# First four heads: operands that stay on their partitions are written by ScalarE instead of copied by DMA

## The chip, the cores and the metric

The kernel runs on one core of a Trainium2 chip. The metric is the time of one execution in microseconds of device time; a kernel's time is the median of several executions. In one core the engines run side by side, each in the order of its own instructions: TensorE (PE, its weight loads shown as PEld), VectorE (DVE), ScalarE (ACT), GpSimd (POOL) and SyncE (SP), which here mainly issues DMA transfers. They wait for one another by semaphores. SBUF, the working memory, and PSUM, into which TensorE writes, have 128 partitions.

## The reference

Three stages follow one another. The change lies in the first, a bucketed attention over 2 batches x 8 heads, 768 positions, head dimension 64:

```python
def _attn_ref(q, k, v, proj):
    q_bits = (einsum('bhsd,dk->bhsk', q, proj) > 0)     # 6 bits
    k_bits = (einsum('bhsd,dk->bhsk', k, proj) > 0)
    mask = q_bucket[:, :, :, None] == k_bucket[:, :, None, :]
    scores = scale * matmul(q, k.transpose(0, 1, 3, 2))
    scores = where(mask, scores, -1e9); scores -= max(scores)
    attn = exp(scores); attn /= attn.sum(-1) + 1e-9
    return matmul(attn, v)
...
def reference(...):
    x = _attn_ref(...)       # 1536 x 512 after the heads are put side by side
    x = _moe_ref(x, ...)     # 8 experts, top 1, 512 -> 1024 -> 512
    return _moe2_ref(x, ...) # 512 -> 2048 -> 512 with a leaky relu
```

## The kernel before

The order of every engine is the order in which the program is written; nothing reorders it. A prologue brings up heads 0, 1 and 2, then a loop of 102 steps runs attention, with the work of later heads spread over its steps by the tables in PLAN (a step runs scores and sums, and at its end the pieces that the tables put there). Then come the experts and the last stage.

Each head has an operand tile OP[h%NP] of 128 partitions x 4 planes x 768 columns; NP is 5, so heads 0 to 3 have a tile that no earlier head used. The scores and the masks come out of it by matmuls over its partitions:

- `load(h)` (L621) brings k and q of a head side by side into `raw[h]`, by two transfers.
- `T(h, half)` (L721) transposes three blocks of 128 positions on TensorE into a PSUM tile `misc` of 128 x 384 (k on partitions 0 to 63, q on 64 to 127). ScalarE writes it, scaled and rounded, to `A[h]` (L728). `T2` (L730) follows at once: VectorE writes the rest, the tile less A, to `B[h]` (L732). There are two `misc` buffers in all, for T, Z, POSTb and a few others.
- `OD(h, n0, n1)` (L738) copies A and B into the operand tile by DMAs that SyncE issues (L617): k's A into planes 0 and 1 of partitions 0 to 63 in one transfer, q's A into plane 2 of partitions 0 to 63 and plane 3 of partitions 64 to 127, k's B into plane 0 of partitions 64 to 127, q's B into plane 3 of partitions 0 to 63. Two of these five, the first and the third, leave the data on the partitions it has; the others move it between the halves.
- `Z` (L742) and, for head 0 alone, `Z0` (L761) compute the bits by three matmuls for each half; VectorE turns them into signs (L755, L769). For Z they go into the operand tile by DMA, for Z0 VectorE writes them there.
- `MAX(u, a)` (L771) is a matmul from planes 2 and 1 and a VectorE reduction (L776) of its row, two for each of the six blocks of a head. `POSTa` and `POSTb` turn the maxima into a row that ScalarE's own DMA queue puts into plane 2 (`op<-mr`, L789).
- `ST(s, a)` (L796) computes the scores by two matmuls (L803, L804), and ScalarE takes the exponential.

GpSimd clears partitions 64 to 127 of planes 1 and 2 of each operand tile ahead (L667, L668).

In the prologue the order is T(0), Z0, T(1), the remaining copies of head 0, MAX of head 0 with Z of head 1 between, POSTa and POSTb, the first ST, T(2), MAX of head 1; T(3) comes at loop step 2, together with Z of head 3 and T(4,0).

Of the kernel before, what the change touches and what calls it, by code (L numbers as in the profile page):

```python
# [13 lines left out]
AF = mybir.ActivationFunctionType  # L14
# [4 lines left out]
SC = 2.0 ** -15  # L19
EPS = 1e-9  # L20
G = 2
NP = 5
# [18 lines left out]
    98, 100, 101), vl=1, am0=(0, 0, 0, 1), Z2=(0, 1), first=(75, 79),  # L41
)
NPRE = 3
NT = 22
NBASE = 13
EH_DVE = ()
# [9 lines left out]
class Router:  # L56
# [5 lines left out]
    def constants(self, w_gate, mbias, mod):  # L62
# [74 lines left out]
        self.rm = P([128, 12], F32, "rm")  # L137
        self.ids = P([128, NT], I32, "ids")
        self.gc = P([128, NT], F32, "gc")
        self.idp = P([128, NPRE], I32, "idp")  # L140
        self.gp = P([128, NPRE], F32, "gp")
        self.did = P([128, 12], I32, "did")
# [153 lines left out]
    def star2(self):  # L296
# [9 lines left out]
        v.tensor_reduce(out=self.m0, in_=k, axis=AX.X, op=ALU.add)  # L306
        v.tensor_scalar(out=self.m0, in0=self.m0, scalar1=128.0 * NPRE, scalar2=None, op0=ALU.min)
        yield
# [15 lines left out]
    def adjust(self, b):  # L324
# [4 lines left out]
        if b == 0:  # L329
            pf = self.tmp([128, 6], F32, "pf")  # L330
            v.scalar_tensor_tensor(out=pf, in0=self.r[:, bs], scalar=128.0 * NPRE, in1=self.isS[:, bs], op0=ALU.is_lt, op1=ALU.mult)
            yield
# [9 lines left out]
    def pre(self, ps):  # L342
# [4 lines left out]
        v.scalar_tensor_tensor(out=q, in0=self.np_[:, 0:6], scalar=100.0, in1=self.rq[:, 0:6], op0=ALU.mult, op1=ALU.add)  # L347
        s = [128, 6, NPRE]
        rc = self.tmp(s, F16, "prc")
        v.tensor_tensor(out=rc, in0=self.iota[:, 0:NPRE].unsqueeze(1).to_broadcast(s), in1=q.unsqueeze(2).to_broadcast(s), op=ALU.is_equal)  # L350
        yield
# [29 lines left out]
    def experts(self):  # L381
# [4 lines left out]
        v.tensor_tensor(out=en, in0=sd[0:1, 0], in1=nt[0:1, 0], op=ALU.add)  # L386
        s = [1, NT, 8]
        it = self.iota[0:1, 0:NT]
        a = self.tmp(s, F32, "xa")
# [4 lines left out]
        v.tensor_tensor(out=a, in0=a, in1=self.iota[0:1, 0:8].unsqueeze(1).to_broadcast(s), op=ALU.mult)  # L394
        et = self.tmp([1, NT], F32, "et")
        v.tensor_reduce(out=et, in_=a, axis=AX.X, op=ALU.add)
        v.tensor_copy(et[:, 0:NPRE], self.es[0:1].to_broadcast([1, NPRE]))
        info = self.info = self.pp.tile([1, 2 * NT + 1], I32, tag="info", name="info")
        v.tensor_copy(info[:, 0:NT], et)
# [74 lines left out]
def _program(base, tc, nc, q, k, v, proj, mod, w_gate, mbias, w1, w2, win, wout, alpha, out):  # L474
# [141 lines left out]
    def f32(ap): return ap.bitcast(F32)  # L616
    def dma32(o,i): nc.sync.dma_start(out=f32(o),in_=f32(i))  # L617
    mm=nc.tensor.matmul
    def misc():
        return ps1.tile([128,512],F32,tag="misc",name="misc",bufs=PS[2])  # L620
    def load(h):  # L621
        b,hh=divmod(h,8)
        t=raw[h]=BIG[2][:,h%3*768:h%3*768+768].rearrange("p (c a d) -> p c a d",c=6,a=2)
        for cs in (slice(0,3),slice(3,6)) if h==0 else (slice(0,6),):
            nc.sync.dma_start(out=t[:,cs,0],in_=k[b,hh].rearrange("(p c) d -> p c d",p=128)[:,cs])
            nc.sync.dma_start(out=t[:,cs,1],in_=q[b,hh].rearrange("(p c) d -> p c d",p=128)[:,cs])
# [20 lines left out]
    for i in range(G):  # L647
        for s in range(2):
            ps=slice(64*s,64*s+64)
            o=pw[ps,i,24*i+12*s:24*i+12*s+12].rearrange("p (a b) -> p a b",a=2)  # L650
# [13 lines left out]
    OP=[]  # L664
    for i in range(NP):
        t=slot16(i)[:,0:3072].rearrange("p (a n) -> p a n",a=4); OP.append(t)
# [45 lines left out]
    def later(f,p):  # L712
        if now[0]: f()
        else: todo.append((p,f))
# [3 lines left out]
    def defer(f,k):  # L718
        if LAGS[k] and not now[0]: dq.append(f)
        else: f()  # L720
    def T(h,half):  # L721
        if half==0:
            A[h]=ep.tile([128,768],F32R,tag="A",name="A",bufs=2); B[h]=ep.tile([128,768],F32R,tag="B",name="B",bufs=2)
        p=misc()
        for c in range(3):
            nc.tensor.transpose(p[:,c*128:(c+1)*128],raw[h][:,half*3+c].rearrange("p a d -> p (a d)"),ident)
        sl=slice(half*384,half*384+384)
        nc.scalar.activation(A[h][:,sl],p[:,0:384],AF.Copy,scale=SC)  # L728
        defer(lambda:T2(h,half,p),0)
    def T2(h,half,p):  # L730
        sl=slice(half*384,half*384+384)
        nc.vector.scalar_tensor_tensor(out=B[h][:,sl],in0=p[:,0:384],scalar=SC,in1=f32(A[h][:,sl]),op0=ALU.mult,op1=ALU.subtract)  # L732
        if half==1:
            if h!=1: OD(h,0,2)
            if h>1:
                OD(h,2,5)
                if 4<h+3<NH: later(lambda:load(h+3),2)
    def OD(h,n0,n1):  # L738
        t=OP[h%NP]; lo,hi=slice(0,64),slice(64,128)
        k2=A[h][lo].unsqueeze(1).to_broadcast([64,2,768])  # L740
        for o,i in (((lo,slice(0,2)),k2),((lo,2),A[h][hi]),((hi,3),A[h][hi]),((hi,0),B[h][lo]),((lo,3),B[h][hi]))[n0:n1]: later(lambda o=o,i=i:dma32(t[o],i),1)
    def Z(hs,half):  # L742
        n=24*len(hs); g=hs[0]
        if half==0: zb[g]=BIG[2][0:24*G,2304:3072]
        p=misc()
        sl=slice(half*384,half*384+384)
        for i,h in enumerate(hs):
            mm(p[0:n,0:384],pwh[:,i,0:n],A[h][:,sl],start=(i==0),stop=False)
            mm(p[0:n,0:384],pwh[:,i,0:n],B[h][:,sl],start=False,stop=False)
            mm(p[0:n,0:384],pwl[:,i,0:n],A[h][:,sl],start=False,stop=(i==len(hs)-1))  # L750
        defer(lambda:Z2(hs,half,p),1)
# [83 lines left out]
    def at(s,f): other.setdefault(s,[]).append(f)  # L835
    def sl_at(s,f): slot.setdefault(s,[]).append(f)
    T(0,0);T(0,1);Z0(0);Z0(1)
    T(1,0);T(1,1)
    OD(0,2,5)
    OD(1,0,2)  # L840
    load(2)
# [10 lines left out]
    for s in ahead[2:]: ST(s,0)  # L852
    load(4)
    T(2,0);T(2,1)
    for u in range(6,NU):
        for a in range(2): MAX(u,a)
# [23 lines left out]
    for s in range(96+LAG+2):  # L880
        us=[u for u in range(nu,min(96,s+6+LA+1,nu+(PLAN["cap"][s] if s<len(PLAN["cap"]) else 2)))]; nu+=len(us)
        fs=dq[:]; dq.clear()
        for o in ORDER:
            t=s-1-LAG
# [13 lines left out]
            t=s-LAG  # L898
# [336 lines left out]
    with ExitStack() as m2:  # L1235
# [64 lines left out]
        for s in range(50):  # L1300
            b, c = divmod(s, 16)
            p = QS[s] if s < 13 else None
# [69 lines left out]
```

## Time and profile before

| | |
|---|---|
| median of 3 runs | 754.55 us (754.51 to 758.52) |
| the profiled execution, its own time | 752.42 us |
| its span, first to last instruction | 750.6 us |
| TensorE busy | 697.3 us, 93% |
| VectorE, ScalarE, GpSimd busy | 69%, 50%, 28% |
| DMA | 83.71 MB, mean 112 GB/s |

An instruction's row in a timeline gives the start, the duration, the engine, the line, the tile written and the tiles read, and in brackets the idle time of the engine ahead of it and what ended it. A row with x2 or more merges instructions that follow one another. The releaser is inferred: where the named one had long been done, it was another, often a transfer. The chain that the profile follows back from the last instruction breaks off at the last transfers and says nothing of this case, so waits were followed by hand.

### The profile page before, as it was taken

To read this page: it belongs to the slowest core of one execution; us is meant where nothing else is said; L and a number is where in the kernel's file an instruction comes from. 1 tells how busy PE (TensorE), PEld (TensorE's weight loads), DVE (VectorE), ACT (ScalarE), POOL (GpSimd) and SP (SyncE) were. 2 spreads that over 40 slices of the span, in tenths; PEclk is the share of its full clock that TensorE was granted. 3 is DMA by queue.
4 is the path that set the end of the run, shared out by engine and by line. 5 is a ranking of instruction groups with operands and counts; after the bars stand their busy time and mean duration, and the time that the engine had idled before them with its cause. 6 is when DMAs were issued, how large, how long until landed. Compare 5 with 4: busy or idle time off the path is not lost. (4 is left out here: it accounts for less than half of the span.)

```text
span 750.6 us, 13216 instructions
## 1 busy us (share of the span) xinstructions
PE 697.3 (93%) x4957; PEld 556.9 (74%) x4957; DVE 518.4 (69%) x959; ACT 372.8 (50%) x666; POOL 207.4 (28%) x178
## 2 busy tenths in 40 slices
PE   6798999999998989899999999898899999999992
PEld 3587888898887777577777767666688888888881
DVE  6788777778879676588879969999963344433430
ACT  1377886887886742356667647555521111111110
POOL 7146786777776420210100021001003010110002
PEclk9779999999999899999999999999999999999997
DMA  7995977667501350355744464543202000010001
GB/s 160 211 188 118 168 205 152 140 174 150 127 12 43 104 206 16 101 169 188 232 142 161 148 213 166 169 168 127 70 1 85 1 28 1 15 42 1 0 1 57
DMA packets 61273, 83.71 MB, mean 112 GB/s; under 512 B 32266, under 2 KB 34410, under 8 KB 60946
## 3 DMA queue, kind: packets, MB, share of 16 engines
q1 hardware_dynamic: 57920, 73.04, 36.0%
q0 software_dynamic: 2960, 9.70, 4.0%
q8 instruction: 41, 0.67, 0.4%
q14 instruction: 30, 0.25, 0.1%
q10 hardware_dynamic: 322, 0.05, 0.0%
HBM read 78.95 MB, written 12.06 MB: 121 GB/s over the span
## 5 line engine op out<-in xcount | busy, mean ns | idle before, releaser
L810 POOL TENSOR_TENSOR El<-E,Eh 128x768 f16<-128x768 f32 x88 | 145.7, 1657 | 86.5 <-ACT Eh L809 67.3
L776 DVE TENSOR_REDUCE mx<-mxp 128x1 f32<-128x384 f32 x189 | 97.7, 550 | 18.6 <-PE mxp L775 18.3
L567 ACT ACTIVATE gh<-gf 128x512 fp32r<-128x512 f32 x48 | 30.3, 631 | 155.9 <-PE o L1280 125.9
L805 ACT ACTIVATE E<-st 128x384 f32<-128x384 f32 x192 | 87.8, 483 | 40.1 <-PE st L804 39.0
L803 PE MATMUL st<-op 97*128 97x384 f32 x192 | 75.4, 393 | 7.5 <-DMA op<-mr 4.5
L570 DVE TENSOR_TENSOR op<-r,op 128x1024 fp32r<-128x1024 f32 (+1 forms) x75 | 77.8, 1080 | 6.3 <-ACT op L567 6.2
L809 ACT ACTIVATE Eh<-E 128x768 f16<-128x768 f32 x96 | 80.2, 836 | 0.0
L567 ACT ACTIVATE op<-r 128x1024 fp32r<-128x1024 f32 (+1 forms) x75 | 65.6, 946 | 13.5 <-DMA r<-in_moe_w_dram 8.6
L775 PE MATMUL mxp<-op 76*128 76x384 f32 x189 | 67.5, 364 | 4.9 <-DVE mx L776 3.2
L570 DVE TENSOR_TENSOR gl<-gf,gh 128x512 fp32r<-128x512 f32 x48 | 33.1, 689 | 54.9 <-ACT gh L567 54.9
L1254 PE MATMUL h<-big,op 128*128 128x512 f32 x256 | 68.6, 395 | 0.7 <-ACT big L1167 0.7
L804 PE MATMUL st<-op 128*128 128x384 f32 x192 | 67.6, 352 | 0.0
L988 PE MATMUL g<-op,xh 128*128 128x512 f32 x156 | 64.4, 467 | 0.0
L1280 PE MATMUL o<-op,gh 128*128 128x512 f32 x192 | 63.4, 391 | 0.0
L818 PE MATMUL av<-vh,Eh 128*128 128x65 f16 x576 | 62.1, 197 | 0.5 <-DVE big L830 0.5
L818 PEld LDWEIGHTS <-Eh 128*128 128x128 f16 x576 | 52.6, 98 | 12.9 <-issue 11.9
L819 PE MATMUL av<-vl,Eh 128*128 128x64 f16 x576 | 61.2, 194 | 0.0
L820 PE MATMUL av<-vh,El 128*128 128x65 f16 x576 | 61.0, 195 | 0.0
L1290 POOL DMA_INDIRECT out_dram<-x,did x12 | 12.2, 1021 | 174.4 <-DVE x L1288 151.2
L1254 PEld LDWEIGHTS h<-big,op 128*128 128x128 f32 x256 | 47.9, 187 | 12.4 <-ACT big L1167 0.9
L1016 PE MATMUL y<-op,hh 128*128 128x512 f32 x156 | 56.8, 429 | 0.0
L1262 DVE TENSOR_SCALAR gf<-h,al 128x512 f32<-128x512 f32 x35 | 26.3, 751 | 41.5 <-PE h L1254 41.3
(388 smaller groups left out, 1580.8 us busy)
## 6 DMA issues: line engine op xcount, KB each, us to landing
r<-in_moe_w_dram SPq DMA_DIRECT2D x42, 768.0 KB
op<-A SPq DMA_DIRECT2D x16, 384.0 KB
op<-A SPq DMA_DIRECT2D x32, 192.0 KB
op<-B SPq DMA_DIRECT2D x32, 192.0 KB
r<-in_moe_w_dram SPq DMA_DIRECT2D x9, 512.0 KB
op<-in_moe_w_in_dram SPq DMA_DIRECT2D x4, 1024.0 KB
op<-in_moe_w_out_dram SPq DMA_DIRECT2D x4, 1024.0 KB
ys<-ysb SPq DMA_DIRECT2D x13, 256.0 KB
```

The lines of the kernel that those rows point to most:

```text
L567: nc.scalar.activation(hi, src, AF.Copy)
L570: eng.tensor_tensor(out=lo, in0=src, in1=f32(hi), op=ALU.subtract)
L775: mm(p[:,0:384],t[0:76,2,c*128:(c+1)*128],t[0:76,1,a*384:a*384+384],start=True,stop=True)
L776: nc.vector.tensor_reduce(out=mx[h][:,c,a:a+1],in_=p[:,0:384],axis=AX.X,op=ALU.max)
L803: mm(p[:,0:384],t[0:97,1,js],t[0:97,2,qs],start=True,stop=False)
L804: mm(p[:,0:384],t[:,0,js],t[:,3,qs],start=False,stop=True)
L805: nc.scalar.activation(E[s][0][:,qs],p[:,0:384],AF.Exp,scale=0.125*2.0**30)
L809: else: nc.scalar.activation(eh,e,AF.Copy)
L810: (nc.vector if s>=ELD else nc.gpsimd).tensor_tensor(out=el,in0=e,in1=eh,op=ALU.subtract)
L818: mm(a[:,c*65:c*65+65],eh[:,cs],VH[h//4%2][:,j,h%4,:],start=(j==0 and c==0),stop=False,skip_group_check=True)
L988: nc.tensor.matmul(p, a[:, ks], b[:, kk, hs], start=False, stop=(kk == 3 and n == 2))
L1254: nc.tensor.matmul(p, terms[t][0][:, kk, cs], terms[t][1][:, kk], start=(n == 0), stop=(n == 11))
```

## The change

For heads 0 to 3 (the new constant NDIR) T writes, behind A, the two operands that stay on their partitions with ScalarE straight out of the PSUM tile into the operand tile, half by half: first k's rows into planes 0 and 1 (64 partitions, 2 x 384 elements, the input read twice), then q's rows into plane 3 (64 partitions, 384). B on VectorE is written behind them in the program. OD leaves out the two transfers for these heads. The other heads are as before.

```diff
 NPRE = 3
+NDIR = 4
 NT = 22
...
         nc.scalar.activation(A[h][:,sl],p[:,0:384],AF.Copy,scale=SC)
+        if h<NDIR:
+
+            t=OP[h%NP]; lo,hi=slice(0,64),slice(64,128)
+            nc.scalar.activation(t[lo,0:2,sl],p[lo,0:384].unsqueeze(1).to_broadcast([64,2,384]),AF.Copy,scale=SC)
+            nc.scalar.activation(t[hi,3,sl],p[hi,0:384],AF.Copy,scale=SC)
         defer(lambda:T2(h,half,p),0)
...
-        for o,i in (((lo,slice(0,2)),k2),((lo,2),A[h][hi]),((hi,3),A[h][hi]),((hi,0),B[h][lo]),((lo,3),B[h][hi]))[n0:n1]: later(lambda o=o,i=i:dma32(t[o],i),1)
+        for o,i in (((lo,slice(0,2)),k2),((lo,2),A[h][hi]),((hi,3),A[h][hi]),((hi,0),B[h][lo]),((lo,3),B[h][hi]))[n0:n1]:
+            if h<NDIR and o in ((lo,slice(0,2)),(hi,3)): continue
+            later(lambda o=o,i=i:dma32(t[o],i),1)
```

## Rows read from the trace of the kernel before

**Rows 1.** Busy time by stretches: stretch, length, engines, granted clock, DMA share, GB/s.
```profile
core 0: us, PE busy (x) PEld busy (x) DVE busy (x) ACT busy (x) POOL busy (x), PEclk, DMA share, GB/s
0.00:12.00 12.00, 6.67 (x26) 3.98 (x27) 6.03 (x19) 3.45 (x6) 8.47 (x22) 1.00 0.68 151
...
24.00:36.00 12.00, 8.23 (x29) 5.82 (x30) 10.97 (x29) 3.81 (x7) 3.24 (x2) 0.74 0.96 201
36.00:46.70 10.70, 10.70 (x39) 8.65 (x40) 7.12 (x13) 6.64 (x14) 3.30 (x2) 0.50 0.96 196
```

**Rows 2.** Timeline of TensorE, 4 to 13 us: start, duration, instruction, idle before.
```profile
6.24 0.55 PE L764 MATMUL misc<-A,p0h 128*44 128x384 f32 x1 [0.59 <-DVE B L732]
...
7.23 0.52 PE L764 MATMUL misc<-A,p0h 128*44 128x384 f32 x1
...
8.88 0.87 PE L726 MATMUL misc<-ident,big 128*128 128x128 f32 x3 [0.49 <-PE misc L766]
10.20 0.87 PE L726 MATMUL misc<-ident,big 128*128 128x128 f32 x3 [0.44 <-DVE op L769]
11.40 0.66 PE L775 MATMUL mxp<-op 76*128 76x384 f32 x1 [0.33 <-POOL op L667]
```

**Rows 3.** Timeline of VectorE, heads 0 and 1.
```profile
5.64 1.13 DVE L732 SCALAR_TENSOR_TENSOR B<-misc,A 128x384 fp32r<-128x384 f32 x2
7.55 2.50 DVE L769 TENSOR_SCALAR op<-misc,tv 12x384 fp32r<-12x384 f32 x4 [0.78 <-PE misc L766]
10.32 0.56 DVE L732 SCALAR_TENSOR_TENSOR B<-misc,A 128x384 fp32r<-128x384 f32 x1 [0.27 <-ACT A L728]
11.63 0.56 DVE L732 SCALAR_TENSOR_TENSOR B<-misc,A 128x384 fp32r<-128x384 f32 x1 [0.76 <-ACT A L728]
12.11 0.55 DVE L776 TENSOR_REDUCE mx<-mxp 128x1 f32<-128x384 f32 x1
```

**Rows 4.** ScalarE: its A's and three back to back, then two groups by form.
```profile
4.92 0.49 ACT L728 ACTIVATE A<-misc 128x384 fp32r<-128x384 f32 x1 [1.44 <-PE misc L726]
...
9.79 0.49 ACT L728 ACTIVATE A<-misc 128x384 fp32r<-128x384 f32 x1 [3.62 <-PE misc L726]
...
22.67 1.08 ACT L728 ACTIVATE A<-misc 128x384 fp32r<-128x384 f32 x2
...
30.20 0.49 ACT L805 ACTIVATE E<-st 128x384 f32<-128x384 f32 x1 [2.19 <-PE st L804]
30.59 0.84 ACT L809 ACTIVATE Eh<-E 128x768 f16<-128x768 f32 x1
31.33 0.48 ACT L805 ACTIVATE E<-st 128x384 f32<-128x384 f32 x1
...
34.76 1.13 ACT L728 ACTIVATE A<-misc 128x384 fp32r<-128x384 f32 x2 [2.22 <-PE misc L726]
...
L567 ACT ACTIVATE op<-r 128x1024 fp32r<-128x1024 f32 x54 | 55.5, 1068 | 5.1 <-DMA r<-in_moe_w_dram 3.0 <-PE y L1016 2.1
L567 ACT ACTIVATE gh<-gf 128x512 fp32r<-128x512 f32 x48 | 30.3, 631 | 155.9 <-PE o L1280 125.9 <-DVE gf L1260 24.9 <-DVE gf L1263 5.2
```

**Rows 5.** Timeline of VectorE, heads 2 and 3.
```profile
23.16 1.17 DVE L732 SCALAR_TENSOR_TENSOR B<-misc,A 128x384 fp32r<-128x384 f32 x2 [3.35 <-ACT A L728]
24.25 3.34 DVE L776 TENSOR_REDUCE mx<-mxp 128x1 f32<-128x384 f32 x7
...
35.28 1.20 DVE L732 SCALAR_TENSOR_TENSOR B<-misc,A 128x384 fp32r<-128x384 f32 x2 [0.51 <-ACT A L728]
```

**Rows 6.** Timeline of TensorE at Z3 and T(4,0).
```profile
35.90 0.52 PE L748 MATMUL misc<-A,pwh 128*24 128x384 f32 x1 [0.53 <-DVE B L732]
...
36.85 0.84 PE L726 MATMUL misc<-ident,big 128*128 128x128 f32 x3
```

**Rows 7.** Timeline of TensorE at the first ST and at T(2).
```profile
19.22 0.41 PE L803 MATMUL st<-op 97*128 97x384 f32 x1 [0.78 <-DMA op<-mr]
...
21.32 0.84 PE L726 MATMUL misc<-ident,big 128*128 128x128 f32 x3
```

**Rows 8.** DMA issues, 0 to 60 us: tile, queue, count, KB each.
```profile
op<-A SPq DMA_DIRECT2D x6, 384.0 KB
op<-A SPq DMA_DIRECT2D x12, 192.0 KB
```

## The prediction

> **What bounds the kernel now.** I read the table by stretches first. From 36 us on TensorE is the bound: 10.70 of 10.70 us busy, and from there to the end of attention it hardly rests [rows 1]. Ahead of it TensorE has 6.67 of 12 us and later 8.23 of 12; there the program is a chain of short steps between engines. From 24 to 36 us VectorE is busy for 10.97 of 12 us. The DMA queues are full (0.96) from 24 us on, which speaks for the change, ScalarE has 3 to 4 us of work in 12. So what the change is worth is read in the first 37 us, and a shift there is carried to the end: what follows is TensorE in program order.
>
> I then followed that chain by the idle time ahead of instructions. Head 0: the transposes of T, ScalarE's A, VectorE's B, the six matmuls of Z0, VectorE's four writes, then the transposes of head 1, which wait for a misc buffer [rows 2, 3]. There are two such buffers, so a transpose or a Z waits until the last reader of the tile two before it is through. Head 1 goes on in the same way, and the first of the MAX reduces starts at 12.11, as the last B ends at 12.19 [rows 3]. For head 2 VectorE sits idle for 3.35 us and waits for A, and TensorE's MAX matmuls are held up behind those two B's [rows 5]. For head 3 it waits again (0.51 us), and TensorE waits for the first B and then needs the buffer of T(3,1) for T(4,0) [rows 5, 6]. In all four heads A and B are on the path. The removed transfers are on it only where a wait names them or the queue: 0.78 us for op<-mr at 19.22 [rows 7], and perhaps the 0.33 us ahead of the first MAX, whose named releaser had nothing to do with it [rows 2].
>
> **What is removed.** For each of four heads one copy of 384 KB and one of 192 KB [rows 8]: 2.36 MB, which at the 201 GB/s of the full stretch [rows 1] is 11.7 us of queue time, and eight issues on SyncE. Few engines wait for it. The 0.78 us may shrink, as the mr transfer then shares the queues with less; bounds 0 to 0.78, I take 0.3. The 0.33 us gives nothing, as the first MAX will be late for another reason. Behind the removed copies on SyncE stand the A[hi] copy of the same head, the B copies and load(2) and so on. They come earlier, or wait for a later A; the load is first used by T(2) at 21.32, for which TensorE does not wait [rows 7]. No gain in either.
>
> **What is added.** In each of eight halves ScalarE writes 64x768 and then 64x384 out of the misc tile, behind A and ahead of the next half's A, and ahead of B in program order. No row has 64 partitions. Conversions to the same type take 631 ns for 512 and 1068 for 1024 elements, so 768 lie at 850 [rows 4]; 384 take 0.49 like A. Back to back the next starts 0.39 us behind a 384 and 0.74 us behind a 768 (starts 30.20, 30.59 and 31.33) [rows 4]. So a half's three writes last 0.39+0.74+0.49 = 1.62 us instead of 0.49 (+1.13), and the next A can start 1.52 us behind the one before. Bounds: without the overlap +1.34; were the 768 to cost only what a 512 does, +0.92. Nothing is gained by itself: ScalarE's added work, 8 x 1.2 us, lies in idle time, but the order counts.
>
> **The open cost: does B wait for the two added readers?** B is written behind them in the program, and all three read the same misc tile. The trace shows no B beside another reader of its tile: all start once A is through, 0.53 us behind A's start [rows 3, 4], and B needs A anyway. So its rows do not settle it. The bounds are no wait (0) and a wait for both (+1.13 per half). I take the wait, because the rows nearest to it, the B's, have both engines strictly one after the other on a tile.
>
> The Trainium skill speaks to this in "PSUM — Partial Sum Buffer", section "PSUM bank collisions raise a hardware error": any two engines that touch one PSUM bank in the same 32 partitions must be ordered, two readers included. B reads all 128 partitions, so by that rule it stands behind both copies; no row of this trace shows two readers without another reason to be ordered. It is the rule that speaks against this change.
>
> **The sum, with the wait.** B then starts 0.53+1.13 = 1.66 us behind A and ends after another 0.56, that is A+2.22; of a pair of halves the second B ends at 1.52+2.22 = 3.74 us behind the first A.
>
> Heads 0 and 1. The first A stays at 4.92, B ends at 7.14, and Z0's first half goes from 6.24 to 7.18, as it needs the buffer. The second A starts at 6.44, its B ends at 8.66 (6.77 now), so Z0's second half goes from 7.23 to 8.70 and ends 1.16 later at 9.86 (8.39 now, by the 0.49 us of idle ahead of 8.88). VectorE's second pair of writes, 1.25 us, ends at 11.23 instead of 10.05. T(1,0) goes from 8.88 to 9.99, T(1,1) from 10.20 to 11.38 [rows 2, 3]. Head 1's first A goes from 9.79 to 10.90 [rows 4], the second can start at 10.90+1.52 = 12.42, its B ends at 14.64 instead of 12.19. The MAX reduces stand behind it on VectorE: **+2.45 us**. They run without a gap to the POSTa's, and ST and T(2) follow from them, so it stays.
>
> Head 2. From the first A at 22.67 to the end of both B's it is 24.33-22.67 = 1.66 us now and 3.74 then: **+2.08 us**. TensorE's MAX matmuls and a full VectorE stand behind [rows 1, 5].
>
> Head 3. The first A is at 34.76. T(4,0) needs the buffer of T(3,1), which is free at 34.76+3.74+0.05 = 38.55 (0.05 for the signal, 0.04 now from the first B's end to 6.24), and it runs at 36.85 now: **+1.70 us**. Z3's first half starts at 37.00 and is through by then [rows 4 to 6]. Behind T(4,0) TensorE is full, so this stays too.
>
> Together 6.23, less 0.3 for mr: +5.9 us. The profiled execution took 752.42 us (750.6 of it span), so 758.3 against it. It lies 2.1 us under the median of the runs, 754.55; against that the forecast is **760.5 us**. The cover: from 36 us on TensorE runs at the lower of its clock levels, 0.50 for 10.7 us [rows 1], and what is late by then finds that level again or not. A third of that stretch at the other level is 10.7/3/2 = 1.8 us, and I put that on both sides.
>
> **The rivals.**
> *B does not wait* (0.15). Then only the next A, and the buffers, held by the copies, are late. The second A at 6.44 and the buffer of T(0,1) free at 6.44+1.62 = 8.06 put Z0's second half at 8.10, VectorE's writes end 0.58 late, head 1's second A is at 11.73 and the last B 0.63 late. Head 2: the second B ends 1.52+0.53+0.56 = 2.61 behind the first A, +0.95. Head 3: T(4,0) is released at 34.76+1.52+1.62+0.05 = 37.95, +1.10. Sum 2.7: 757.2 us, no change that can be told. For it: no row shows such a wait. Against: the order of the program.
>
> *The queues are the bound* (0.06), faster. If the chain were set by the transfers, taking out 11.7 us of queue time would give up to 11.7 back, less the added work: at best 743 us, 749 with half of it. For it: a share of 0.96 from 24 us on. Against: once the first load is there, the longest wait of TensorE in the first 37 us that names a transfer is this 0.78 us [rows 7]. It decides from where the waits for op copies exceed the 6.2 us added; visible ones come to a sixth.
>
> *The delay is swallowed* (0.07), 754 to 756 us. The low clock from 36 us could end earlier in absolute time than the shift suggests, and give back 10.7/2 = 5.35 us, were all of it at the full clock. For it: TensorE is full there, so the clock is worth that much. Against: nothing in the change makes TensorE busier ahead of it; it has more idle time.
>
> **How the numbers follow.** The forecast has 0.72. Its own range is 757.5 to 764: down by 1.8 us of clock and some of mr, up by 1.2 us were there no overlap on ScalarE (0.2 us in six halves on the path), mr giving nothing, and 1.8 us of clock. The range reaches down to the first rival with half a microsecond of relief and some clock: **756 to 764**. A measurement tells 0.5%, 3.8 us, from no change, so slower begins at 758.3. Of the forecast 0.86 lies above, of the first rival a quarter, of the last none: slower 0.66. Faster 0.06. Same 0.28.
>
> **What the profile after would show.** Behind each A of heads 0 to 3 stand two more ScalarE rows, of about 0.85 and 0.49 us, and B's start moves from 0.53 to about 1.66 us behind A's. If it stays at 0.53, the first rival holds. The first MAX reduce moves from 12.11 to about 14.6, the reduces behind head 2's B's from 24.25 to about 28.5, and the full stretch of TensorE from 36 to about 42. The bytes that the queues move up to 48 us fall by 2.36 MB, and the wait for mr at the first ST shrinks. The prediction is wrong if the first ST (19.22 now) comes earlier than now: then the queues did bind, or if it comes 2.4 us later and the full stretch still starts near 36: then VectorE had slack between 24 and 36 that its busy time does not show. If all shifts are as told and the end is not, the clock made the rest.

## The result and the profile after

The changed kernel takes 764.34 us, median of 8 runs (762.94 to 766.56). The kernel before takes 757.92 us, median of 8 (754.51 to 759.35); the three runs that were known ahead are among them, and the five others alone have 758.39. The ratio is 1.0111, 95% interval 1.0083 to 1.0140: slower, by 6.4 us if the medians are subtracted and by 8.4 us by the ratio. The forecast was slower by 5.9 us. Its number, 760.5, and its range, up to 764, lie too low, for the most part because they stand on the median of the three runs (754.55), 3.4 us below that of the eight.

ScalarE in the changed kernel, heads 0 and 1, answers to the first rows of [rows 4] (start, duration, instruction, idle time before and what ended it):

```profile
4.95 0.49 ACT L729 ACTIVATE A<-misc 128x384 fp32r<-128x384 f32 x1 [1.47 <-PE misc L727]
5.34 0.79 ACT L733 ACTIVATE op<-misc 64x768 fp32r<-64x768 f32 x1
6.14 0.48 ACT L734 ACTIVATE op<-misc 64x384 fp32r<-64x384 f32 x1
6.65 0.49 ACT L729 ACTIVATE A<-misc 128x384 fp32r<-128x384 f32 x1
...
11.20 0.49 ACT L729 ACTIVATE A<-misc 128x384 fp32r<-128x384 f32 x1 [2.87 <-PE misc L727]
```

VectorE, the same heads and heads 2 and 3, answers to [rows 3, 5]:

```profile
6.66 0.56 DVE L738 SCALAR_TENSOR_TENSOR B<-misc,A 128x384 fp32r<-128x384 f32 x1 [0.84 <-ACT op L734]
8.36 0.56 DVE L738 SCALAR_TENSOR_TENSOR B<-misc,A 128x384 fp32r<-128x384 f32 x1 [1.14 <-ACT op L734]
8.95 2.50 DVE L777 TENSOR_SCALAR op<-misc,tv 12x384 fp32r<-12x384 f32 x4
12.91 0.56 DVE L738 SCALAR_TENSOR_TENSOR B<-misc,A 128x384 fp32r<-128x384 f32 x1 [1.46 <-ACT op L734]
14.61 0.56 DVE L738 SCALAR_TENSOR_TENSOR B<-misc,A 128x384 fp32r<-128x384 f32 x1 [1.14 <-ACT op L734]
15.08 0.55 DVE L784 TENSOR_REDUCE mx<-mxp 128x1 f32<-128x384 f32 x1
...
27.82 0.56 DVE L738 SCALAR_TENSOR_TENSOR B<-misc,A 128x384 fp32r<-128x384 f32 x1 [5.24 <-ACT op L734]
29.52 0.56 DVE L738 SCALAR_TENSOR_TENSOR B<-misc,A 128x384 fp32r<-128x384 f32 x1 [1.14 <-ACT op L734]
30.00 3.33 DVE L784 TENSOR_REDUCE mx<-mxp 128x1 f32<-128x384 f32 x7
...
43.85 0.56 DVE L738 SCALAR_TENSOR_TENSOR B<-misc,A 128x384 fp32r<-128x384 f32 x1 [1.14 <-ACT op L734]
```

Each B now waits for `op`, the second added write (L734), and no longer for A: it starts 1.71 us behind A (6.66 against 4.95) where it was 0.53. The MAX reduces begin at 15.08 instead of 12.11. TensorE, as in [rows 6, 7]:

```profile
22.43 0.66 PE L811 MATMUL st<-op 97*128 97x384 f32 x1 [0.97 <-DMA op<-mr]
...
24.80 0.84 PE L727 MATMUL misc<-ident,big 128*128 128x128 f32 x3
...
42.77 0.52 PE L756 MATMUL misc<-A,pwh 128*24 128x384 f32 x1 [2.03 <-DVE B L738]
...
44.47 0.90 PE L727 MATMUL misc<-ident,big 128*128 128x128 f32 x3 [0.55 <-DVE B L738]
```

The first ST comes 3.2 us later, T(4,0) 7.62 us. The transfers did get lighter. The stretch from 12 to 48 us, first before, then in the changed kernel (stretch, length, engines, granted clock, DMA share, GB/s):

```profile
12.00:48.00 36.00, 30.46 (x137) 22.42 (x136) 27.82 (x66) 14.38 (x30) 11.88 (x15) 0.72 0.96 203
```

```profile
12.00:48.00 36.00, 25.71 (x82) 17.80 (x81) 23.27 (x57) 16.12 (x32) 8.41 (x12) 0.90 0.61 143
```

The share of the queues falls from 0.96 to 0.61. Part of that is only the delay: in the kernel below that has the same delay and keeps every transfer it is 0.83. In those 36 us TensorE gets through 82 matmuls instead of 137, though its granted clock is higher, and VectorE through 57 rows instead of 66. A resource was relieved that the chain did not wait for.

How far the two kernels are apart along the program: the start of one and the same VectorE row, less its start in the first profile of before. The rows are those at 12.11, about 36, 100, 227.5, 251.4, 304.7 and 735.3 us of before; the other columns are kernels of the next section.

```
row at (us)  changed  before again  writes+transfers  tiny rows  behind pair (1st, 2nd)
  12.1         2.98       0.25           2.92            0.16        -0.16  -0.23
  36           7.93       0.49           8.08            0.89         0.39   0.62
 100           5.52      -0.70           6.22           -0.44        -0.90  -1.55
 227.5         6.61      -0.11           7.15            0.59        -0.72  -1.42
 251.4        10.33      -0.12           9.32            2.75         0.92   1.70
 304.7        10.68       2.40          12.10            4.75         0.40   2.70
 735.3        13.90       2.90          13.72            4.90         2.55   6.59
```

The cost is there in full by 36 us. By 100 us 2.4 us of it seem to be given back, but the second profile of before gains 1.2 us on the first there itself; against the second, the changed kernel is 7.4, 6.2 and 6.7 us late at 36, 100 and 227.5 us. Behind 227 us the profiles drift apart again, those of one and the same program too. The first profile of before (752.42 us) is among its quickest runs and that of the changed kernel (766.13 us) among its slowest, so the last line overstates what the change costs: 13.9 us in the profiles, 6.4 to 8.4 in the runs.

### The profile page after: what moved, and what is told of

Its sections match the earlier page's. It is cut to its first block, busy times and chain, and to the rows that moved or that the text cites. A ratio compares the mean times of both kernels' runs of the same rounds, so it can differ in the third digit from the quotient of the medians.

```text
span 764.4 us, 13231 instructions
## 1 busy us (share of the span) xinstructions
PE 700.5 (92%) x4957; PEld 558.9 (73%) x4957; DVE 519.7 (68%) x959; ACT 381.8 (50%) x682; POOL 207.4 (27%) x178
```

## The experiments

The theory after the result: B is ordered behind the two added readers of its PSUM tile, this and the later next A put 7 us into the first 45 us, and the removed transfers give nothing back. The rivals: ScalarE's added time alone; transfers that do count; something behind 227 us. The kernels and where T(4,0) starts in each (36.85 in the first profile of before), with the ratio to before:

```
                                              T(4,0)   ratio (95%)
the kernel before, again                       37.49   0.998 (0.995 to 1.001)
the changed kernel                             44.47   1.011 (1.008 to 1.014)
writes from A in SBUF, same place              40.87   1.007 (1.004 to 1.010)
writes from A, behind the pair of halves       37.40   1.004 (1.001 to 1.008)
  the same again                               37.47   1.004 (1.001 to 1.006)
B ahead of the writes, all from PSUM           45.12   1.012 (1.009 to 1.016)
the change for heads 0 and 1                   40.35   1.006 (1.003 to 1.010)
the change for heads 2 and 3                   41.71   1.012 (1.008 to 1.016)
added writes to scratch, all transfers kept    44.62   1.010 (1.007 to 1.014)
El on VectorE from step 72 on                  44.55   1.018 (1.009 to 1.028)
before and eight tiny ScalarE rows             37.73   1.003 (1.000 to 1.005)
scratch writes behind the pair, transfers kept 38.06   1.005 (1.002 to 1.007)
```

**The kernel before, again.** No edit.

> The kernel before, once more, to see how far two executions of one program lie apart and in which stage. Theory (the added ScalarE rows ahead of B cost some 7 us in the first 45 us, and whatever else the first two profiles differ by comes from stages that differ from one execution to the next): ratio 1.000, first MAX reduce within 0.2 us of 12.11, T(4,0) within 0.3 us of 36.85, but up to 7 us of difference to the first profile in the stages behind 225 us. Rival (the change also costs time behind 225 us): the stages behind 225 us lie within 1 us of the first profile of before.

T(4,0) differs by 0.64 us, more than the 0.3 allowed for, the first MAX reduce by 0.25. Up to 251 us the two profiles of before stay within 1 us of each other, then the second falls 2.5 us behind. So a profile can be read to about a microsecond up to there, and not to two behind it. The stretch between the rows at 251.4 and 304.7 us, in the first profile and then in the second:

```profile
251.41:304.69 53.28, 50.58 (x469) 39.54 (x470) 37.63 (x99) 24.17 (x48) 9.08 (x7) 1.00 0.34 115
```

```profile
251.29:307.09 55.80, 53.48 (x469) 42.03 (x470) 37.56 (x98) 24.43 (x48) 9.07 (x7) 0.94 0.32 110
```

TensorE runs the same 469 matmuls, but is busy for 2.9 us more, at a mean granted clock of 0.94 instead of 1.00, and idle for 2.3 us instead of 2.7. So the 2.5 us are matmuls at the lower of its two levels (1.2 GHz), not a longer wait. In the changed kernel the same stretch takes 53.63 us at 0.96; in the kernel with writes to scratch and all transfers 56.05 us at 0.93. Why the clock falls there in one execution and not in another is not shown.

**Writes from A in SBUF.** Only the source differs, so B has no other reader of its PSUM tile.

```diff
-            nc.scalar.activation(t[lo,0:2,sl],p[lo,0:384].unsqueeze(1).to_broadcast([64,2,384]),AF.Copy,scale=SC)
-            nc.scalar.activation(t[hi,3,sl],p[hi,0:384],AF.Copy,scale=SC)
+            nc.scalar.activation(t[lo,0:2,sl],f32(A[h][lo,sl]).unsqueeze(1).to_broadcast([64,2,384]),AF.Copy)
+            nc.scalar.activation(t[hi,3,sl],f32(A[h][hi,sl]),AF.Copy)
```

> The two added writes stand where they stand, but read A in SBUF instead of the PSUM tile, so that B has no other reader of its tile ahead of it. Theory (two thirds of the cost is B's wait behind the two writes): B starts 0.53 us behind A instead of 1.7; the second A still starts 1.70 behind the first. Last B of head 1 ends at 12.7, of head 2 1.1 us later than before against its A, T(4,0) +2.4 us against before (39.3) instead of +7.6; ratio 1.003. Rival (ScalarE's time alone, that is the later next A, is the cost): T(4,0) as late as in the changed kernel, 44 us, ratio 1.010.

Head 2, VectorE and then ScalarE:

```profile
24.49 0.56 DVE L737 SCALAR_TENSOR_TENSOR B<-misc,A 128x384 fp32r<-128x384 f32 x1 [3.96 <-ACT A L729]
26.41 0.56 DVE L737 SCALAR_TENSOR_TENSOR B<-misc,A 128x384 fp32r<-128x384 f32 x1 [1.36 <-ACT A L729]
```

```profile
23.99 0.46 ACT L729 ACTIVATE A<-misc 128x384 fp32r<-128x384 f32 x1
24.49 0.84 ACT L732 ACTIVATE op<-A 64x768 fp32r<-64x768 f32 x1
25.34 0.52 ACT L733 ACTIVATE op<-A 64x384 fp32r<-64x384 f32 x1
25.88 0.49 ACT L729 ACTIVATE A<-misc 128x384 fp32r<-128x384 f32 x1
```

B starts with the first added write, 0.50 us behind A: without a second reader of the PSUM tile there is no wait. T(4,0) is +4.0 us instead of +7.6, so up to there the order on the tile is about half the cost and the later next A the other half. By 227.5 us this kernel is only 1.2 us behind the first profile of before, the changed kernel 6.6; in the runs it is 1.007, where I had expected 1.003. My +2.4 was too low in part because the second A starts 1.89 us behind the first here, not 1.70: the first added write starts 0.50 instead of 0.39 us behind A, and the two last 0.84 and 0.52 us instead of 0.79 and 0.48.

**B ahead of the writes.** The two added lines stand behind `defer(lambda:T2(h,half,p),0)`, and all three read PSUM.

> B is written ahead of the two added writes in the program; all three read the PSUM tile. Theory (two engines that read one PSUM tile are ordered as the program has them): B starts 0.53 us behind A, the two writes start only as B has ended, 1.3 us behind A, the next A starts 2.6 us behind the one before instead of 1.7, and the buffer is free 2.6 us behind A; T(4,0) 8 to 9 us later than before, ratio 1.010 to 1.012. Rival (only VectorE is held, or the two run side by side): the first added write starts 0.4 us behind A while B runs, T(4,0) +2.7 us, ratio 1.003.

```profile
26.34 0.46 ACT L729 ACTIVATE A<-misc 128x384 fp32r<-128x384 f32 x1
27.43 0.80 ACT L733 ACTIVATE op<-misc 64x768 fp32r<-64x768 f32 x1 [0.62 <-DVE B L737]
28.24 0.49 ACT L734 ACTIVATE op<-misc 64x384 fp32r<-64x384 f32 x1
28.75 0.49 ACT L729 ACTIVATE A<-misc 128x384 fp32r<-128x384 f32 x1
```

Now ScalarE waits for B, though it needs nothing that B writes. In this program two engines that read one PSUM tile are put one after the other in the order in which it is written, whichever is first. The next A starts 2.41 us behind, T(4,0) is +8.3 us. The theory holds; and putting B first is no gain, since the next A is then late.

**The parts.** The change with NDIR = 2, and the change with `h in (2,3)` in place of `h<NDIR`.

> The change for heads 0 and 1 alone. Theory (each head's chain carries its own part): first MAX reduce at 15.1 as in the changed kernel (+3.0 us), head 2's last B 3.2 to 3.5 us later than before instead of 5.75, T(4,0) at 40.0 to 40.4 (+3.3); ratio about 1.004. Rival (VectorE or the low clock swallows a shift of 3 us by 37 us, and only the four heads together show): T(4,0) within 1 us of 36.85, ratio 1.000.

> The change for heads 2 and 3 alone. Theory: the first MAX reduce stays at 12.1, head 2's last B is 2.3 us later than before, T(4,0) 4.2 us (41.0); ratio about 1.005, and the two halves of the change add up to the whole. Rival (the prologue's part is the whole cost, as in the loop ScalarE and VectorE have slack): T(4,0) within 1 us of 36.85, ratio 1.000.

T(4,0) is +3.5 and +4.9 us against the first profile of before, +2.9 and +4.2 against the second; the whole is +7.6 and +7.0. At T(4,0) the parts add up, and little of a shift of 3 us is swallowed: against the second profile, 2.2 of the 2.9 and 3.5 of the 4.2 us are left at 227.5 us. The ratios don't add up: 0.6% and 1.2% against 1.1% for the whole. That of heads 2 and 3 alone (1.012, six runs) is more than its chain explains (3.4 us, 0.4%); its interval reaches down to 0.8%. That of heads 0 and 1 (1.006) is also above its chain's 2.1 us, 0.3%; its interval reaches down to 0.3%.

**The transfers kept.** From the kernel before; the added writes go to a scratch tile that nothing reads.

```diff
+        if h<4:
+            lo,hi=slice(0,64),slice(64,128)
+            nc.scalar.activation(SCR[lo],p[lo,0:384].unsqueeze(1).to_broadcast([64,2,384]),AF.Copy,scale=SC)
+            nc.scalar.activation(SCR[hi,0],p[hi,0:384],AF.Copy,scale=SC)
```

> The two added ScalarE writes go into a scratch tile that nothing reads, and all transfers of before stay. What differs from the changed kernel is only whether the two transfers of each head are there. Theory (the transfers are worth nothing on the path): T(4,0) within 0.5 us of the changed kernel's 44.47, ratio to before 1.009 to 1.012 as for the changed kernel. Rival (the removed transfers give back part of the cost): T(4,0) 1 us or more behind 44.47 and a ratio above 1.013.

T(4,0) at 44.62 against 44.47, ratio 1.010 against 1.011: with or without the 2.36 MB of transfers the same, as far as the intervals tell (0.4%). The wait for mr at the first ST, with all transfers:

```profile
22.42 0.66 PE L808 MATMUL st<-op 97*128 97x384 f32 x1 [1.02 <-DMA op<-mr]
```

It was 0.78 before and 0.97 with the transfers removed. It doesn't follow the load of the queues.

**Behind the pair.** If neither A nor B has an added write ahead of it, the transfers' worth stands alone.

```diff
         defer(lambda:T2(h,half,p),0)
+        if h<NDIR and half==1:
+            t=OP[h%NP]; lo,hi=slice(0,64),slice(64,128)
+            nc.scalar.activation(t[lo,0:2],f32(A[h][lo]).unsqueeze(1).to_broadcast([64,2,768]),AF.Copy)
+            nc.scalar.activation(t[hi,3],f32(A[h][hi]),AF.Copy)
```

> The two added writes come from A in SBUF and only behind the second half's A and B, in one piece for 768 columns; the DMAs stay removed. Nothing is then ahead of any A or B of the same head. Theory: the path is that of before, T(4,0) within 0.5 us of 36.85, ratio 0.998 to 1.001, and what it lies below 1 is the whole worth of the removed transfers (at most the 0.78 us wait for op<-mr and 1.5 us of VectorE behind op<-big). Rival (the transfers were a bound that the added wait hid): T(4,0) 3 us or more earlier than before, ratio below 0.996.

> The kernel whose added writes come from A behind the pair of halves, once more. Its first ratio, 1.0044, lay above what its own trace showed up to 227 us (0.7 us ahead of before). Theory (executions of any of these kernels differ by some 5 us in the stages behind 225 us and around the low clock before 60 us, so a ratio of one comparison is no finer than 0.3%): ratio 1.000 to 1.004, T(4,0) within 0.6 us of 36.85 again. Rival (this form costs 3 us in a place that the first trace did not show): ratio 1.004 to 1.006 again, and a stage ahead of 225 us that is 2 us or more longer.

T(4,0) is back at 37.4 and 37.5, the chain stands 0.7 and 1.4 us ahead of before at 227 us: that is all the transfers can be worth. Yet both ratios are 1.004, some 3 us slower, and neither interval reaches down to 1. Ahead of the first run neither the theory nor the rival had this; for the repeat I had put it down to the spread of the executions (1.000 to 1.004), which a second ratio as high speaks against.

**What costs 3 us behind 227 us.** First the VectorE rows of 128x6 and 128x8, the router's, beside GpSimd, which computes El there (the exponentials less their f16 part Eh). The changed kernel, VectorE and then GpSimd:

```profile
246.00 1.61 DVE L313 TENSOR_SCALAR selm<-sel,m 128x8 f32<-128x8 f32 x1
...
247.53 1.70 DVE L317 TENSOR_SCALAR so<-iota,es 128x8 f32<-128x8 f32 x1
...
253.68 0.17 DVE L258 CAST si<-rp 128x6 int32<-128x6 f32 x1
253.89 1.56 DVE L260 TENSOR_SCALAR qi<-si 128x6 int32<-128x6 int32 x1
...
255.49 1.56 DVE L261 TENSOR_SCALAR si<-si 128x6 int32<-128x6 int32 x1
...
258.39 1.38 DVE L217 TENSOR_SCALAR gs<-gs 128x6 f32<-128x6 f32 x1
```

```profile
253.77 3.25 POOL L818 TENSOR_TENSOR El<-E,Eh 128x768 f16<-128x768 f32 x2 [2.79 <-PE st L812]
```

The row at 253.89, of six elements, lasts 1.56 us instead of 0.17, up to the end of the El that began just ahead of it, and the next one up to the end of the second El. The changed kernel and the other kernels up to here have five such rows of over 1 us between 225 and 262 us; before has three, in both of its profiles. In the first:

```profile
237.85 1.62 DVE L312 TENSOR_SCALAR selm<-sel,m 128x8 f32<-128x8 f32 x1
239.38 1.69 DVE L316 TENSOR_SCALAR so<-iota,es 128x8 f32<-128x8 f32 x1
...
247.47 1.40 DVE L216 TENSOR_SCALAR gs<-gs 128x6 f32<-128x6 f32 x1
```

To see whether GpSimd is the cause, El goes to VectorE from step 72 on, in the changed kernel.

```diff
-ELD = 88
+ELD = 72
```

> The changed kernel, with GpSimd's subtractions (El) moved to VectorE from step 72 on instead of step 88. Question: in the changed kernel's trace VectorE rows of 128x6 and 128x8 between 245 and 260 us last 1.4 to 1.7 us instead of 0.17 to 0.25, each as long as one El row of GpSimd beside it; before has three of them between 235 and 250 us, the changed kernel five. Theory (VectorE's short writes in SBUF stand still while GpSimd's subtraction runs, and how many are hit depends on how far the two chains are apart): with no El on GpSimd there, no row of 128x6 or 128x8 lasts over 0.5 us in that stretch; VectorE takes some 16 x 1.03 us for the El's instead, so the time may go either way by 5 us. Rival (transfers or the low clock hold VectorE): some rows of 128x6 or 128x8 still last over 1 us. The chain up to 200 us is as in the changed kernel: T(4,0) within 0.5 us of 44.47.

The two rows, now without an El on GpSimd (line, form, count, busy us, mean ns of one, idle before):

```profile
L260 DVE TENSOR_SCALAR qi<-si 128x6 int32<-128x6 int32 x1 | 0.2, 174 | 0.0
L261 DVE TENSOR_SCALAR si<-si 128x6 int32<-128x6 int32 x1 | 0.2, 171 | 0.0
```

No such row lasts over 0.25 us in that stretch. So El on GpSimd holds them. As a whole this kernel gains nothing: 1.018 (1.009 to 1.028) from two runs, which is not told from the changed kernel's 1.011. Its chain is already 9.8 us late at 227.5 us, where that of the changed kernel is 6.6; that VectorE's own El's do this is argued, not shown.

Then whether any small edit changes what happens there: the kernel before with rows that do next to nothing, and with the added work behind the pair, but every transfer kept.

```diff
+        if h<4 and half==1:
+            for i in range(2): nc.scalar.activation(SCR[i],one[:,0:1],AF.Copy)
```

> The kernel before with eight ScalarE rows of 8x1 (0.2 us each) behind the second half of T for heads 0 to 3, into tiles that nothing reads; all transfers stay. It asks where the 0.4% of the form with the writes behind the pair comes from, whose traces are not later than before up to 227 us. Theory (a small shift of the chains against one another decides how often VectorE's short rows meet GpSimd's El behind 225 us, and how the waits behind 250 us fall, so any small change can be worth some 3 us there): ratio 1.000 to 1.004, T(4,0) within 0.7 us of 36.85, and behind 225 us a count of drawn-out short rows other than before's three. Rival (only real work or missing transfers cost): ratio 0.998 to 1.001 and the same rows as before behind 225 us.

> As the form with the added writes behind the pair of halves, but they go into a scratch tile (in two pieces each) and all transfers of before stay: ScalarE's work alone, off the path. Theory (neither the work nor the missing transfers cost by themselves; the stages behind 227 us do): T(4,0) within 0.7 us of 37.4, ratio within 0.004 of that form's 1.004, either way. Rival A (the missing transfers cost there): ratio 0.998 to 1.001. Rival B (ScalarE's work costs there): ratio 1.0035 or more.

The tiny rows give 1.003, with an interval that just reaches no change. Their profile has five drawn-out rows instead of three and falls 2.2 us behind between 227 and 251 us:

```profile
246.34 1.54 DVE L259 TENSOR_SCALAR qi<-si 128x6 int32<-128x6 int32 x1
247.91 1.56 DVE L260 TENSOR_SCALAR si<-si 128x6 int32<-128x6 int32 x1
```

These are the two rows that the changed kernel has and before has not. The shift of VectorE's rows against before steps up by 1.4 us at each of them, with the tiny rows from 0.59 to 3.36 us and in the changed kernel from 8.16 to 10.93, and 0.6 us is given back by 251 us. With the work behind the pair and all transfers kept the ratio is 1.005, as without them. So the missing transfers don't cost behind 227 us; a shift of under a microsecond between the chains is enough to bring two more short rows behind an El. In some of the other kernels it is two other short rows. The number of such rows does not settle the whole loss: the kernels with five lose between 1.6 and 3.7 us from 227 to 251 us, and heads 0 and 1 alone 6.5 us, at a granted clock of 0.69 there. How much of the 0.1 to 0.2% between the tiny rows and the work behind the pair is ScalarE's work, and what else lengthens the stretch from 305 to 335 us (by 3.4 us in the profile of the changed kernel), is open. No form tried is faster than the kernel before.

## Why the prediction was right and where it failed

The direction, the mechanism and the place were right: VectorE's B waits behind the two added writes, in all four heads, and this moves a chain that nothing covers up to 227 us. The sum was 5.9 us; the chain stands 7.6 us late at T(4,0) and 6.6 at 227 us (7.0 and 6.7 against the second profile of before), and the runs give 6.4 to 8.4.

The step that failed is the level: "against that the forecast is 760.5 us". I added the difference to 754.55, the median of three runs from 754.51 to 758.52, as if it were firm. The eight runs have 757.92. Of the 3.8 us between 760.5 and 764.34 the level makes 3.4 and the difference 0.5; with 5.9 us on top of 757.9 the forecast would have been 763.8. The level is not the same in every set of runs: beside the experiments the kernel before has 757.95 (29 runs), 758.23 (23), 755.52 (21) and 755.37 (3). That two of the three runs agreed to 0.04 us told nothing of the third, 4 us away. The range allowed for the clock, the overlap on ScalarE and mr, and nothing for the level.

The difference was too small as well, and 763.8 would have come so near by some luck: 5.9 us on 754.55 is a ratio of 1.0078, just under the interval of the measured one (1.0083 to 1.0140). What it lacks is the overlap on ScalarE, the wait for mr, and a term for what happens behind 227 us.

The terms of the sum:

- A half's writes. Forecast 1.52 us from one A to the next, measured 1.70 (6.65 against 4.95). The 64x768 takes 0.79 us instead of 0.85, and the first overlap of 0.1 us is there, but the two others are not: the 64x384 starts 0.80 us behind the 64x768 and the next A 0.51 us behind that. From the first A of a pair to the end of the second B it is 3.94 us (26.14 to 30.08) instead of 3.74.
- Heads 0 and 1: +2.45 forecast, +2.97 measured at the first MAX reduce. Head 2: +2.08, and 3.94-1.66 = 2.28. Head 3: +1.70, and 1.93 (T(4,0) moves by 7.62, its first A from 34.76 to 40.45). All are low by the same overlap that wasn't there. Together they make 7.2 of the 7.6 us.
- The wait for mr: 0.3 us of gain forecast, none measured; it grew by 0.2, to 0.97 us.
- The clock: 1.8 us allowed to either side, none seen in the first 62 us. The profile of the changed kernel has a mean granted clock of 0.92 there, that of the kernel with El on VectorE, the same program up to there, 1.00; they stand 6.8 and 6.9 us behind before.
- "The open cost": the wait of 1.13 us was taken, against none. Measured, B moves from 0.53 to 1.71 us behind A, by 1.18, and with another source the wait is gone. The choice was right, though the rows that it stood on, each B behind its A, had another reason to be ordered. The Trainium skill, "PSUM — Partial Sum Buffer", section "PSUM bank collisions raise a hardware error", has two readers of one bank ordered as well; here the trace agrees, in both directions: B waits 0.84 and 1.14 us for ScalarE, and with B first ScalarE waits 0.62 us for B.
- The rivals. "B does not wait" put T(4,0) 2.7 us late, against 7.6. "The queues are the bound" fell with the kernel that keeps all transfers. "The delay is swallowed": against the second profile of before, of 7.0 us at T(4,0) 6.2 are left at 100 us and 6.7 at 227.5.
- Not in the sum at all: what a shift does behind 227 us, some 2 to 3 us through short VectorE rows held by GpSimd, and, from one execution to another, some 2 us through the granted clock. I took TensorE's program order as a promise that a shift is carried on unchanged.

## What to carry to other kernels

Before a second engine's copy is taken out of a PSUM tile, ask who else reads that tile: here readers on two engines stood in line, in program order. Putting B first did not help (45.12 against 44.47 at T(4,0)), since the next A on ScalarE then came late; a copy in SBUF as the source took away B's wait, and only added work behind the whole pair left the chain where it was. A queue that was full over a stretch was worth nothing to relieve here, since hardly a wait on the chain ended with its transfers; look for the waits, not for the share. And time the kernel before often enough to know its spread before a difference of one per cent is put on top of it.

## What the runs showed of the hardware that was not expected

GpSimd's subtraction of 128x768 with both inputs in SBUF (1.65 us) holds some VectorE rows of 128x6 and 128x8 that only touch SBUF until it ends: in before and in the changed kernel 1.4 to 1.7 us instead of 0.15 to 0.23. VectorE's MAX reduces out of PSUM keep their 0.55 us. The Trainium skill tells of this in "SBUF — State Buffer", section "Who interferes with whom": some VectorE forms and GpSimd share a pair of ports, and whoever comes second waits for the whole instruction. The rows agree with that, and the kernel without El on GpSimd in that stretch has none of them there.

On ScalarE, a write that reads PSUM starts 0.39 us behind an A of 0.49 us, but one that reads in SBUF what the A has just written starts 0.50 to 0.53 us behind it. That is no rule for every such pair: Eh, which reads the E just written, starts 0.39 us behind it in [rows 4].
